# Setting the sign of the converted float64 weights in ScalarE's scaled copy instead of in a third VectorE operation

## The chip, the cores and the metric

The kernel runs on one core of one Trainium2 chip. The metric is the device time of one execution in microseconds. Engines are called by the profile's names: PE (matrix multiplies), DVE (vector), ACT (scalar, activations), POOL (GpSimd) and SP (here only a queue that issues transfers).

## The reference

The inputs `q`, `k`, `v`, `p` are float32, all weights are float64. What is computed, cut to its core:

```python
p_packed = sm_attn(p, k, v)                    # 8 x 8 heads, 32 packed rows, 576 keys, head size 64
x = sm_attn(q, p_packed, p_packed)             # then 4608 tokens x 512
g = x @ w_gate                                 # 512 -> 1536
x = (g * (1 / (1 + exp(-g))) * (x @ w_val)) @ w_out      # 1536 -> 512
return (((x @ w1) * (x @ w2)) @ w3) @ w_out2   # 512 -> 1024 -> 1024 -> 512
```

`sm_attn` scales by 1/8, subtracts the row's maximum, takes the exponential and divides by the row's sum plus 1e-9.

## The kernel before, in words

The program has four stages. **Front** (to about 111 us): sixteen units, one for each batch and half of the heads, load `k` and `v`, transpose on PE, and make the packed rows; its order is written out by hand as tasks at fractions of a unit (`task`, `run`), and each engine runs its part in that order. **P = 0** (to about 250 us): the first of four batch pairs; twelve steps `f`, each with the gate and value products of 128 columns (`stage1`, lines 440 to 473), a combination of weights with packed rows (`c_mm`, tile `pc`, then `ch` and `cl`), and after each third step the output product (`stage3`, tiles `px` and `acc`). **P = 1 to 3** (to about 840 us): the same steps with weights that were stored to DRAM; in P = 3 the products `w3 @ w_out2` (`w3_T`, `w3_mm`) are put between. **Tail**: the second MLP. From the front's end on, a scheduler sets each engine's order by its own estimate of when work is ready, so an instruction can move when another is shortened or goes away.

[...] `conv` (line 334) turns each tile of 128 x 512 numbers into float32 from its two 32-bit words, `high` and `low`. ACT multiplies `high`, taken as a float32, by 2^-112 (L347), into the target tile `t`; DVE shifts `low` right by 29 into `x` (`vx`, L350); DVE shifts `t` left by 3 and joins `x` (L357). The shift throws the sign away. It is put back in one of two ways: behind the front by DVE with the top bit of `high` (L360), and in the front by an ACT `Sign` (L354) and a POOL multiplication (L363), spread over two later times of the hand-written order (`CVD`).

There are 76 such tiles: `w` (gate and value, 24, target `wf`), `wo` (12, target `wof`), `w12` (16), `wo2` (8) and `w3` (16, targets `vt`). Six of them, `wf` 0 to 2, are converted in the front, 24 + 12 - 6 = 30 in P = 0 or just ahead of it, the rest later. In P = 0, `c_mm` of step `f` needs `wf` of step `f`, which is converted two steps ahead. The raw tiles have five buffers; a load on the SP queue waits until a buffer's last reader is done.

Of the kernel before, what the change touches and what calls it, by code (L numbers as in the profile page):

```python
# [8 lines left out]
F32 = mybir.dt.float32  # L9
F32R = mybir.dt.float32r  # L10
I32 = mybir.dt.int32
I64 = mybir.dt.int64
AF = mybir.ActivationFunctionType
ALU = mybir.AluOpType
# [5 lines left out]
VD = 0  # L20
RAW0 = (7, 8, 10, 11, 12, 13, 15, 15, 15, 16.75)
WS = {10.0: (0, 0), 11.0: (0, 1), 13.25: (1, 0), 14.25: (1, 1), 15.25: (2, 0), 16.25: (2, 1)}
CVD = (0.25, 1.25)
SPD = 2.25
CS = (13, 16)
CO = (14.0, 17.0)
# [4 lines left out]
QD = ((0, 'load'), (4.0, 'T'), (5.25, 'mm'), (6.0, 'max'), (6.0, 'sub', 'pool'), (6.75, 'exp'), (7.25, 'sum'), (7.75, 'div', 'pool'), (8.75, 'aT', 'later'), (9.5, 'split'))  # L31
STD = 4.75
W3B = 5
DSIGN = ('w',)
SIGN = -(1 << 31)
W3S = ((0, 1, 2, 3), (1, 3), (1, 3))
NPS = 0

# [2 lines left out]
def packed_attention_moe_kernel(  # L41
# [24 lines left out]
    nc = tc.nc  # L66
# [16 lines left out]
    scale = 1.0 / float(D) ** 0.5  # L83

    def pool(name, side, bufs=1, **kw):
        return tc.alloc_tile_pool(name=name, bufs=bufs, side=side, reuse_waits="tile", **kw)
# [30 lines left out]
    vc = pool("vc", "left", bufs=2)  # L117
# [18 lines left out]
    in_front, conv_rest, pin, pin_at = [True], [], {}, {}  # L136
    NO_SYNC = mybir.DependencyInfo(mybir.DependencyClass.NoSync, mybir.DependencyReason.DATA)

    def behind(x, what):
        if what in pin:  # L140
            tc.add_manual_dep(x.ins, pin[what].ins.name, NO_SYNC, reason="behind the last unit")
# [176 lines left out]
    def raw_load():  # L318
        if raw_at[0] < len(raw_q):
            key = raw_q[raw_at[0]]  # L320
            src = raw_src(key)
            raw_at[0] += 1
            blocks = src.shape[0] == 4
            t = vc.tile([128, 512] if blocks else [128] + list(src.shape[1:]), I64, tag="raw",
                        name=f"raw_{key}", bufs=5)
            if blocks:
                for i in range(4):
                    to = t[32 * i:32 * i + 32]
                    nc.sync.dma_start(to if len(src.shape) == 3 else to.rearrange("p (r n) -> p r n", r=4), src[i])
            else:  # L330
                nc.sync.dma_start(t, src)
            raw_t.append((key, t))

    def conv(key, t):


        name, raw = raw_t.pop(0)
        assert name == key, (name, key)
        x = vc.tile(list(t.shape), I32, tag="vx", name=f"vx_{key}")
        w = raw.bitcast(I32)  # L340
        if len(t.shape) == 3:
            w = w.rearrange("p a (n e) -> p a n e", e=2)
            low, high = w[:, :, :, 0], w[:, :, :, 1]
        else:
            w = w.rearrange("p (n e) -> p n e", e=2)
            low, high = w[:, :, 0], w[:, :, 1]
        behind(nc.scalar.activation(t, high.bitcast(F32), AF.Copy, scale=2.0 ** -112), "act")  # L347
        dve = not in_front[0] and key.startswith(DSIGN)
        sg = None if dve else vc.tile(list(t.shape), F32, tag="sg", name=f"sg_{key}")
        behind(nc.vector.tensor_scalar(x, low, 29, None, op0=ALU.logical_shift_right), "dve")  # L350

        def sign():
            if not dve:
                nc.scalar.activation(sg, high.bitcast(F32), AF.Sign)  # L354

        def rest():
            nc.vector.scalar_tensor_tensor(  # L357
                x, t.bitcast(I32), 3, x, op0=ALU.logical_shift_left, op1=ALU.bitwise_or)
            if dve:
                nc.vector.scalar_tensor_tensor(  # L360
                    t.bitcast(I32), high, SIGN, x, op0=ALU.bitwise_and, op1=ALU.bitwise_or)
            else:
                nc.gpsimd.tensor_tensor(out=t, in0=x.bitcast(F32), in1=sg, op=ALU.mult)  # L363

        if in_front[0]:
            conv_rest.extend((sign, rest))
        else:
            sign()
            rest()
        if not in_front[0]:  # L370
            raw_load()
# [4 lines left out]
    def w_conv(f, gv):  # L376
        if gv == 0:
            wf_t[0, f] = wst_t[f] = wgv.tile([128, 4, 2, 128], F32, tag=("wh", "wl")[f % 2], name=f"wf0_{f}")
        t = wf_t[0, f]
        conv(f"w_{f}_{gv}", t[:, :, gv, :])  # L380
# [11 lines left out]
    def wo_conv(f):  # L392
        t = vl.tile([128, DM], F32, tag="vt", name=f"wof0_{f}")
        conv(f"wo_{f}", t)
        wof_t[0, f] = t
# [123 lines left out]
    def pa_s(u):  # L519


        kT = kT_t.pop(u)
        t = psum(f"psp{u}")
        for hq in range(4):
            for e in range(2):
                es = slice(64 * e, 64 * e + 64)
                nc.tensor.matmul(
                    t[hs[hq], e, 0:HS].rearrange("j (m p g) -> j g m p", m=3, g=3), lhsT=kT[es, 9, hs[hq]],
                    rhs=kT[es, 0:9, hs[hq]].rearrange("d (g m) p -> d g m p", g=3), start=True, stop=True, tile_position=(64 * e, 32 * hq))
        mx = pa.tile([128, 1], F32, tag="mx", name=f"mx{u}")  # L530
        nc.vector.reduce_max(mx, t[:, :, 0:HS], axis=AX.XY)
        nc.vector.tensor_scalar_mul(mx, mx, -scale)
        return t, mx
# [57 lines left out]
    def task(s, fn, *args):  # L591
        extra.setdefault(s, []).append((fn, args))
# [7 lines left out]
        task(s, raw_load)  # L600
    for s, (f, gv) in WS.items():
        task(s, w_conv, f, gv)
        for d in CVD:
            task(s + d, lambda: conv_rest.pop(0)())
    C_t["later"] = [None]
    for f in range(2):
        task(CS[f] + 0.5, c_mm, 0, f)
# [10 lines left out]
    with tc.manual_schedule(engines=M0):  # L618
        for s in range(last + 1):
# [6 lines left out]
            if 0 <= s - 1 < U:  # L626
                x = pa_s(s - 1)
# [61 lines left out]
    def w12_conv(i):  # L689
        x, c, h = w12_list[i]  # L690
        t = vl.tile([128, 512], F32, tag="vu", name=f"w12t{i}")
        conv(f"w12_{i}", t)
        nc.sync.dma_start(
            w12d[4 * h:4 * h + 4, :, x, c, :].rearrange("f p n -> p f n"),
            t.rearrange("p (f n) -> p f n", n=128))
# [408 lines left out]
```

## Time and profile before

| | us |
|---|---|
| median of 3 runs | 1408.45 (1404.53 to 1416.2) |
| the profiled execution, its own time | 1409.99 |
| its span, first to last instruction | 1408.2 |
| PE busy | 1356.6 (96%) |
| DVE busy | 715.9 (51%) |
| ACT busy | 577.0 (41%) |
| POOL busy | 400.6 (28%) |

Busy times are sums over the whole span, and the stages have different limits; the granted clock of PE was 0.99 of full speed in the mean. A matmul row's length depends on that clock, so a stretch of half clock shows as longer rows, not as idle time.

### The profile page before, as it was taken

How to read it: one execution, taken by the hardware profiler on the slowest of the kernel's cores; microseconds unless marked ns; L12 is line 12 of the kernel's file. 1: busy time of each engine (PE TensorE's matmuls, PEld its weight loads, DVE VectorE, ACT ScalarE, POOL GpSimd, SP SyncE). 2: the span in 40 equal slices, each digit the busy share in tenths (PEclk: the TensorE clock that was granted, in tenths of full speed). 3: DMA queues.
4: the chain of work that ended last, by engine and by line, in shares of the span. 5: the costliest groups of instructions: out<-in, count | busy, mean ns of one | idle time of the engine just before them, and what ended most of it. 6: DMA issues, size and time to landing. Idle time of an engine off the chain costs nothing.

```text
span 1408.2 us, 25693 instructions
## 1 busy us (share of the span) xinstructions
PE 1356.6 (96%) x10228; PEld 1243.6 (88%) x10228; DVE 715.9 (51%) x1016; ACT 577.0 (41%) x946; POOL 400.6 (28%) x315
## 2 busy tenths in 40 slices
PE   7779989999999999999999989999999999999998
PEld 5557988999999999998988889989999899898997
DVE  3557769536584566664265467933323323334130
ACT  5585525435243353354453234623323323233231
POOL 0244223332223323254243334602212022021120
PEclk9999999999999999999999999999999999999999
DMA  9997567543446534235442137946728458185451
GB/s 255 252 253 195 196 177 238 137 154 85 137 107 179 174 101 135 59 118 153 133 145 88 61 109 254 337 167 195 224 85 254 148 162 253 59 252 174 133 158 45
DMA packets 188871, 230.28 MB, mean 164 GB/s; under 512 B 70736, under 2 KB 119888, under 8 KB 188752
## 3 DMA queue, kind: packets, MB, share of 16 engines
q1 hardware_dynamic: 188752, 228.64, 54.6%
q8 instruction: 81, 1.33, 0.4%
q14 instruction: 38, 0.31, 0.1%
HBM read 179.04 MB, written 49.55 MB: 162 GB/s over the span
## 4 chain that ended last, share of the span: by engine, by line
PE 77%; DVE 8%; DMA 6%; issue 4%; ACT 3%; POOL 1%; SPq 0%; DVEq 0%; ACTq 0%; POOLq 0%
PE px L668 19%; PE po L1041 14%; PE pA L977 12%; PE pg L454 8%; PE pv L454 8%; PE pB L977 6%; PE pC L977 3%; PE pc L422 3%; DMA km<-in_k_dram 2%; PE pw L732 1%; DMA raw_w<-in_moe_w_val_dram 1%; PE pk L512 1%; DVE vx_w L357 1%; DVE ws L90 1%; PE psq L207 1%
## 5 line engine op out<-in xcount | busy, mean ns | idle before, releaser
L90 POOL TENSOR_TENSOR ul<-u,uh 128x576 fp32r<-128x576 f32 x96 | 153.7, 1601 | 344.5 <-ACT uh L94 333.0
L997 POOL TENSOR_TENSOR c<-s,s 128x384 f32<-128x384 f32 x48 | 49.2, 1025 | 375.9 <-ACT s L992 375.7
L668 PE MATMUL px<-uh,woh 128*128 128x384 f32 x576 | 147.6, 336 | 3.2 <-DVE acc L678 2.2
L668 PE MATMUL px<-ul,woh 128*128 128x384 f32 x576 | 147.3, 336 | 2.6 <-POOL ul L90 2.6
L668 PE MATMUL px<-uh,wol 128*128 128x384 f32 x576 | 146.9, 336 | 0.0
L992 ACT COPY s<-pA 128x384 f32<-128x384 f32 x144 | 69.2, 481 | 181.7 <-PE pA L977 179.2
L463 DVE TENSOR_TENSOR u<-u,pv 128x576 f32<-128x576 f32 x96 | 71.8, 748 | 97.7 <-PE pv L454 83.2
L94 ACT CAST uh<-u 128x576 fp32r<-128x576 f32 x96 | 64.7, 674 | 134.7 <-DVE u L463 134.7
L1041 PE MATMUL po<-wo_hi,abl 128*128 128x512 f32 x288 | 112.3, 390 | 0.2 <-DVE abl L90 0.2
L1041 PE MATMUL po<-wo_lo,abh 128*128 128x512 f32 x288 | 112.2, 389 | 0.0
L1041 PE MATMUL po<-wo_hi,abh 128*128 128x512 f32 x288 | 112.0, 389 | 0.0
L668 PEld LDWEIGHTS px<-uh,woh 128*128 128x128 f32 x576 | 103.2, 188 | 5.9 <-DVE acc L678 2.8
L678 DVE TENSOR_TENSOR acc<-acc,px 128x768 f32<-128x768 f32 x72 | 68.1, 948 | 77.4 <-PE px L668 77.2
L668 PEld LDWEIGHTS px<-ul,woh 128*128 128x128 f32 x576 | 104.5, 188 | 3.1 <-POOL ul L90 3.1
L668 PEld LDWEIGHTS px<-uh,wol 128*128 128x128 f32 x576 | 104.6, 189 | 0.0
L90 DVE TENSOR_TENSOR abl<-ab,abh 128x768 fp32r<-128x768 f32 x48 | 48.1, 1003 | 105.1 <-ACT abh L94 105.1
L90 POOL TENSOR_TENSOR wol<-wof,woh 128x512 fp32r<-128x512 f32 x48 | 63.7, 1340 | 99.6 <-ACT woh L94 86.2
L454 PE MATMUL pg<-aTh,ch 128*128 128x288 f32 x384 | 87.9, 310 | 2.2 <-ACT u L459 2.2
L454 PE MATMUL pv<-aTh,ch 128*128 128x288 f32 x384 | 83.3, 299 | 2.9 <-ACT u L459 2.6
L459 ACT ACTIVATE u<-pg 128x576 f32<-128x576 f32 x96 | 62.3, 649 | 54.1 <-PE pg L454 53.2
L454 PE MATMUL pv<-aTl,ch 128*128 128x288 f32 x384 | 82.8, 298 | 0.0
L454 PE MATMUL pg<-aTh,cl 128*128 128x288 f32 x384 | 82.8, 297 | 0.0
(312 smaller groups left out, 3190.4 us busy)
## 6 DMA issues: line engine op xcount, KB each, us to landing
ws<-wsd SPq DMA_DIRECT2D x245, 256.0 KB, 3.0
wf<-Wd SPq DMA_DIRECT2D x36, 512.0 KB, 4.5
wsd<-ws SPq DMA_DIRECT2D x49, 256.0 KB, 3.5
km<-in_k_dram SPq DMA_DIRECT2D x16, 576.0 KB, 12.7
wof<-wod SPq DMA_DIRECT2D x36, 256.0 KB, 3.2
x2r<-X2d SPq DMA_DIRECT2D x24, 384.0 KB, 5.2
out_dram<-o SPq DMA_DIRECT2D x36, 256.0 KB, 2.0
raw_w<-in_moe_w_dram SPq DMA_DIRECT2D x16, 512.0 KB, 4.9
```

The lines of the kernel that those rows point to most:

```text
L90: return eng.tensor_tensor(out=out, in0=src, in1=hi.bitcast(F32), op=ALU.subtract)
L94: nc.scalar.copy(hi, src)
L422: nc.tensor.matmul(t[hs[at], b, Q], lhsT=PTd[es, 2 * (2 * P + b) + Q, hs[hq]], rhs=w[es, 2 * Q + hq // 2].rearrange("p g n -> p (g n)"), s ...
L454: nc.tensor.matmul(t[:, hf, 0:HS], lhsT=w[:, b % 2, Q, cols], rhs=x[:, Q, hf, :], start=first, stop=last,)
L459: x = nc.scalar.activation(u, t[:, :, 0:HS], AF.Silu)
L463: x = nc.vector.tensor_tensor(out=u, in0=u, in1=t[:, :, 0:HS], op=ALU.mult)
L668: nc.tensor.matmul(t[:, h, 0:CW], lhsT=w[:, 128 * d:128 * d + 128], rhs=x[:, CW * c:CW * c + CW], start=first, stop=last,)
L678: nc.vector.tensor_tensor(out=o, in0=o, in1=t[:, :, 0:CW], op=ALU.add)
L977: nc.tensor.matmul(bk[n], lhsT=w[:, hl, 128 * d:128 * d + 128], rhs=r[:, d], start=(first and d == 0 and i == 0), stop=(d == 1 and i == 2) ...
L992: nc.scalar.copy(o, t)
L997: on.tensor_tensor(out=r, in0=o, in1=t, op=op)
L1041: nc.tensor.matmul(t, lhsT=a[:, j, cols], rhs=w[:, f], start=first, stop=last)
```

## The change

ACT's scaled copy becomes a `Prelu` with slope -2^32. A positive high word gives the same as before. A negative one gives its magnitude, 32 binades up: bit 28 of the word is then set, and the shift left by 3 moves it to the sign's place. The third DVE operation, the `Sign` and the POOL multiplication are gone, as are the tiles `sg`; the joining operation now writes `t` in place. In the front it stands a quarter of a unit behind its load's task, where before it stood one and a quarter behind.

```diff
-CVD = (0.25, 1.25)
+CVD = 0.25
...
-        behind(nc.scalar.activation(t, high.bitcast(F32), AF.Copy, scale=2.0 ** -112), "act")
-        dve = not in_front[0] and key.startswith(DSIGN)
-        sg = None if dve else vc.tile(list(t.shape), F32, tag="sg", name=f"sg_{key}")
+        behind(nc.scalar.activation(t, high.bitcast(F32), AF.Prelu, scale=2.0 ** -112, alpha=-2.0 ** 32), "act")
         behind(nc.vector.tensor_scalar(x, low, 29, None, op0=ALU.logical_shift_right), "dve")
-
-        def sign():
-            if not dve:
-                nc.scalar.activation(sg, high.bitcast(F32), AF.Sign)
 
         def rest():
             nc.vector.scalar_tensor_tensor(
-                x, t.bitcast(I32), 3, x, op0=ALU.logical_shift_left, op1=ALU.bitwise_or)
-            if dve:
-                nc.vector.scalar_tensor_tensor(
-                    t.bitcast(I32), high, SIGN, x, op0=ALU.bitwise_and, op1=ALU.bitwise_or)
-            else:
-                nc.gpsimd.tensor_tensor(out=t, in0=x.bitcast(F32), in1=sg, op=ALU.mult)
+                t.bitcast(I32), t.bitcast(I32), 3, x, op0=ALU.logical_shift_left, op1=ALU.bitwise_or)
 
         if in_front[0]:
-            conv_rest.extend((sign, rest))
+            conv_rest.append(rest)
         else:
-            sign()
             rest()
...
-        for d in CVD:
-            task(s + d, lambda: conv_rest.pop(0)())
+        task(s + CVD, lambda: conv_rest.pop(0)())
```

In all, the DVE has 70 instructions fewer, ACT six and POOL six; the number of activation table loads in the program is 16 before and after. PE's order is the same. Two places of the order matter below. First DVE in P = 0, between `wf` of step 6 and `wf` of step 7 (`cl` is the remainder of `pc`, `aT` and `aTl` belong to the attention of the next batch). Before:

```order
L360 SCALAR_TENSOR_TENSOR wf_6_2272<-raw_w_1_2023,vx_w_1_2280 128x4x128
L350 TENSOR_SCALAR vx_wo_2320<-raw_wo_2030 128x512
L463 TENSOR_TENSOR u_4_2288<-u_4_2288,pv_4_2303 128x576
L357 SCALAR_TENSOR_TENSOR vx_wo_2320<-wof_4_2319,vx_wo_2320 128x512
L261 STREAM_TRANSPOSE aT_0_2636<-sT_1947 128x576
L360 SCALAR_TENSOR_TENSOR wof_4_2319<-raw_wo_2030,vx_wo_2320 128x512
L90 TENSOR_TENSOR cl_6_2351<-pc_6_2333,ch_6_2350 128x1024
```

And in the changed kernel, the same stretch:

```order
L349 SCALAR_TENSOR_TENSOR wf_6_2244<-wf_6_2244,vx_w_1_2251 128x4x128
L449 TENSOR_TENSOR u_4_2211<-u_4_2211,pv_4_2226 128x576
L346 TENSOR_SCALAR vx_wo_2290<-raw_wo_2003 128x512
L88 TENSOR_TENSOR aTl_2598<-aT_0_2599,aTh_2597 128x576
L349 SCALAR_TENSOR_TENSOR wof_4_2289<-wof_4_2289,vx_wo_2290 128x512
L449 TENSOR_TENSOR u_4_2258<-u_4_2258,pv_4_2273 128x576
L259 STREAM_TRANSPOSE aT_1_2603<-sT_1922 128x576
L88 TENSOR_TENSOR aTl_2598<-aT_1_2603,aTh_2597 128x576
L88 TENSOR_TENSOR cl_6_2320<-pc_6_2302,ch_6_2319 128x1024
```

The two L360 are gone. Both `aTl` and the second `aT`, which stood behind `wf` of step 7, now stand ahead of it; the first `aT` moved further up, ahead of `cl` of step 5.

Second, ACT somewhat earlier in P = 0, at the exponential of the next batch's attention (`sT`), among the output copies `acc` of the first `stage3`. Before:

```order
L674 COPY acc_3_2174<-px_0_3_2155 128x768
L94 CAST woh_3_2136<-wof_3_2127 128x512
L674 COPY acc_4_2195<-px_0_4_2176 128x768
L239 ACT_TABLE_LOAD
L239 ACTIVATE sT_1947<-sT_1947 128x1152
```

In the changed kernel:

```order
L659 COPY acc_3_2146<-px_0_3_2127 128x768
L92 CAST woh_3_2108<-wof_3_2100 128x512
L237 ACT_TABLE_LOAD
L237 ACTIVATE sT_1922<-sT_1922 128x1152
L659 COPY acc_4_2167<-px_0_4_2148 128x768
```

The table load and the exponential moved ahead of one `acc` copy.

## Rows read from the trace of the kernel before

**Rows 1.** Stretches: us, each engine's busy time (instructions), PE clock, DMA share, GB/s

```profile
250.00:574.00 324.00, 324.00 (x2811) 302.57 (x2810) 194.73 (x230) 132.53 (x190) 102.40 (x71) 1.00 0.48 135
...
180.00:185.00 5.00, 4.46 (x43) 3.34 (x44) 4.85 (x8) 2.73 (x4) 2.56 (x2) 0.50 0.87 278
```

**Rows 2.** Timeline of PE: start, length, instruction, [idle before it, and what ended that]

```profile
130.06 1.16 PE L207 MATMUL psq<-qT,PTd 64*32 64x288 f32 x12 [0.41 <-DVE qT L158]
132.86 1.10 PE L422 MATMUL pc<-wf,PTd 64*32 64x256 f32 x32 [1.64 <-DVE wf L360]
...
169.26 1.10 PE L422 MATMUL pc<-wf,PTd 64*32 64x256 f32 x32 [1.01 <-DVE wf L360]
...
180.53 1.96 PE L422 MATMUL pc<-wf,PTd 64*32 64x256 f32 x32 [3.58 <-DVE wf L360]
...
228.95 1.10 PE L422 MATMUL pc<-wf,PTd 64*32 64x256 f32 x32 [1.54 <-DVE wf L360]
...
647.07 0.53 PE L454 MATMUL pv<-aTh,ch 128*128 128x288 f32 x2 [2.58 <-ACT u L459]
...
716.19 0.53 PE L454 MATMUL pg<-aTh,ch 128*128 128x288 f32 x2 [2.23 <-ACT u L459]
...
744.04 0.62 PE L668 MATMUL px<-uh,woh 128*128 128x384 f32 x2 [1.94 <-DVE acc L678]
```

**Rows 3.** The chain that ended last, PE's pieces: start, length, what

```profile
182.50 3.18 PE pg L454 x12
185.68 2.10 PE pv L454 x12
...
197.16 1.60 PE pg L454 x12
...
647.07 2.93 PE pv L454 x12
```

**Rows 4.** Groups by line and shape: count | busy us, mean ns | idle before

```profile
L360 DVE SCALAR_TENSOR_TENSOR wf<-raw_w,vx_w 128x512 int32<-128x512 int32 x18 | 13.2, 751 | 0.0
L357 DVE SCALAR_TENSOR_TENSOR vx_w<-wf,vx_w 128x512 int32<-128x512 int32 x24 | 17.7, 753 | 0.1
L347 ACT ACTIVATE wf<-raw_w 128x512 f32<-128x512 f32 x24 | 15.6, 673 | 6.1 <-DMA raw_w<-in_moe_w_gate_dram 5.0 <-DMA raw_w<-in_moe_w_val_dram 1.1
L354 ACT ACTIVATE sg_w<-raw_w 128x512 f32<-128x512 f32 x6 | 4.0, 675 | 0.0
L459 ACT ACT_TABLE_LOAD x8 | 10.3, 1283 | 2.7 <-PE pg L454 2.6
```

**Rows 5.** Stretches, line L360 alone: us, DVE busy (instructions), PE clock, DMA

```profile
111.30:132.90 21.60, 3.93 (x6) 1.00 0.56 154
160.80:180.50 19.70, 3.88 (x5) 0.98 0.53 158
215.80:229.00 13.20, 2.72 (x4) 1.00 0.71 220
634.00:647.00 13.00, 2.16 (x2) 1.00 0.56 178
```

**Rows 6.** Timeline of DVE and ACT in P = 0

```profile
157.21 1.94 DVE L234 TENSOR_TENSOR sT<-sT,qmx 128x1152 f32<-128x1152 f32 x1
...
159.66 1.17 ACT L239 ACTIVATE sT<-sT 128x1152 f32<-128x1152 f32 x1
...
182.18 0.74 DVE L90 TENSOR_TENSOR aTl<-aT,aTh 128x576 fp32r<-128x576 f32 x1
```

**Rows 7.** Timeline of DVE and ACT late in the front

```profile
94.04 0.68 DVE L357 SCALAR_TENSOR_TENSOR vx_w<-wf,vx_w 128x512 int32<-128x512 int32 x1
...
94.62 0.69 ACT L347 ACTIVATE wf<-raw_w 128x512 f32<-128x512 f32 x1
```

**Rows 8.** The chain that ended last, in P = 3

```profile
733.30 1.96 DVE vt_w L360
...
737.12 3.59 DMA raw_w<-in_moe_w_dram
```

More of the change, by code (lines that the diff above doesn't have):

```diff
@@ L33 @@
 W3B = 5
-DSIGN = ('w',)
-SIGN = -(1 << 31)
 W3S = ((0, 1, 2, 3), (1, 3), (1, 3))
```

## The prediction, as it was put on record

> **What bounds the kernel now.** I read the stretches first, to see where PE is ever idle; then PE's timeline for each gap and what ended it; then the chain of waits backwards from each gap, to see whether a removed operation is on it. PE bounds the program: from 250 to 574 us it is busy 324.00 of 324.00 us [rows 1]. Nothing that is taken from DVE there can show in the time. What a change of DVE can win is PE's gaps, and there are few. Eight of them matter [rows 2]. Four are ended by L360 itself, the operation that goes: 1.64, 1.01, 3.58 and 1.54 us, each the matmul `pc` that waits for `wf`, all in P = 0. One of 0.41 us stands just before the first, behind a DVE transpose in the same rush. Three are in P = 3: 2.58 us and 2.23 us ended by ACT's `u`, 1.94 us ended by DVE's `acc`. In P = 0 DVE is the late engine, while elsewhere it has room.
>
> A gap costs more than its length when the clock drops behind it. Behind the 3.58 us gap the stretch 180 to 185 was granted 0.50 of full speed [rows 1], the lower of the two levels: `pc` took 1.96 us where others take 1.10 [rows 2], and the twelve matmuls of `pg` and `pv`, 1.60 us at full speed, took 3.18 and 2.10 us [rows 3]. That is 0.86 + 1.58 + 0.50 = 2.94 us on top. Behind the 2.58 us gap `pv` took 2.93 us, 1.33 more than 1.60 [rows 3]. Behind the 1.54 us gap `pc` took the usual 1.10 us [rows 2].
>
> **The change part by part.** *The third DVE operation goes.* 70 of them, 0.751 us each in the form of `wf` [rows 4], some 52 us of DVE time; only what lies on the way to one of the gaps counts.
>
> (a) 130 to 133 us, idle 0.41 + 1.64 = 2.05 us. Between the front's end and this gap DVE runs six L360, 3.93 us [rows 5]. Part of that is hidden where DVE waits for ACT, but the two of them for `wf` of step 4 lie behind those waits and the `wof` pair is what ACT itself waits for. I take the gap as closed: 2.05 us.
>
> (b) 169 and 180.5 us, idle 1.01 + 3.58 = 4.59 us. The stretch begins with the end of the exponential (159.66 + 1.17 us [rows 6]), and from there DVE has no pause until the second gap ends. Five L360 go, 3.88 us [rows 5]. The exponential itself comes earlier: DVE's subtraction ahead of it ends at 157.21 + 1.94 = 159.15 us [rows 6] and has two L360 ahead of it (2 x 0.68, taken with the shortest price, 0.68 us, as L357 had at 94.04 us [rows 7]: 1.36), and ACT no longer does one `acc` and the table load between. So it starts near 157.8, not 159.66: 1.8 us. Against that, the order puts two `aTl` and one `aT` ahead of `wf` of step 7: three operations near 0.74 us [rows 6], 2.2 us. Net 3.88 + 1.8 - 2.2 = 3.4 us of the 4.59; some 1.2 us of idle time stays. As a gap of 1.54 us kept the full clock, I take the 2.94 us of slow clock as gone. Together 6.3 us.
>
> (c) 229 us, idle 1.54 us. Four L360, 2.72 us, between 215.8 and 229 us [rows 5]; the first stands behind a load's landing and the others behind each other. Closed: 1.54 us.
>
> (d) 647 us, idle 2.58 us and 1.33 us of clock, 3.91 us. Two L360 with 2.16 us lie between 634 and 647 us [rows 5]; through `acc` and its store they hold the SP queue, on which the load of `wof` stands, which ACT's cast and then `u` wait for. The scheduler has moved casts and loads here too, so I take half: 2.0 us.
>
> (e) 744 us, idle 1.94 us. A raw load landed here after 3.59 us [rows 8]; its buffer came free when L360 at 733.30, 1.96 us long, had read `high` [rows 8]. Now the last readers are the Prelu and the shift, which stand earlier than L360, so the load starts at least that much sooner. Closed: 1.94 us.
>
> (f) 716 us, idle 2.23 us: the way there goes over POOL's `w3l` and the one buffer of `w3T`, not over L360. Nothing.
>
> *Prelu for Copy.* The trace of before has no Prelu. Nearest are the same shape as scaled copy, 0.673 us, and as `Sign`, 0.675 us [rows 4], the latter a function that also treats the two signs apart. I take 0.675; 76 x 0.002 us is nothing. *The joining operation in place.* It reads what L357 reads and writes where L360 wrote: 0.753 and 0.751 us [rows 4], no difference. *Front.* Six `Sign` (4.0 us on ACT [rows 4]) and six POOL products go; the joining operation stands a unit earlier. The front hangs on its loads and ACT, so I take nothing for it either way.
>
> Sum: 2.05 + 6.3 + 1.54 + 2.0 + 1.94 = 13.9 us. Against the profiled execution's 1410.0 that is **1396**; this execution stands 1.5 us above the median of the runs shown.
>
> **The rivals.** *Everything closes*: (b) and (d) in full, 2.05 + 4.59 + 2.94 + 1.54 + 3.91 + 1.94 = 17.0, and perhaps (f): 1391 to 1393. Chance 0.09.
>
> *New waits take the old ones' place*, chance 0.27. With DVE early, the next late ones are ACT's casts and `u` and the loads of raw tiles. For it: the long gaps (b) and (d) have several engines on their way, and the order moved there. Against it: ACT was busy 2.73 of 5 us in the worst stretch [rows 1]. Only (a), (c) and (e) are won: 1410 - 5.5 = 1404.5.
>
> *The change frees nothing*: the gaps stay in other names, 1410 within 2 us. Against it speaks that four gaps name L360 itself. Chance 0.06.
>
> *The front gets slower*, the other side. The joining operation now follows its Prelu within the unit. Where DVE comes to it before ACT has done the Prelu, DVE stands, and the maximum or the sum's reciprocal and `Pd` of the packed rows stand behind it, which PE waits for. In the trace DVE would be there at 94.04 us, the copy ended at 94.62 + 0.69 = 95.31 [rows 7]: 1.3 us. If all six tiles lost that on the path, 7.6 us; if also nothing were won later, 1418. It decides when ACT lags in most of the six, and by the rows it lags in that one. Chance 0.04. With the later gains it gives 1404.
>
> *Table loads*, also slower. If Prelu were not in the function table that is active, each one between exponentials or Silus would need a load and a load back, 1.283 us each [rows 4]: for the six of the front, where ACT is the tight engine, 6 x 2.57 = 15 us, 1425, and more in P = 0. It decides with the count of loads, and the program has 16 before and after. Chance 0.02. [...]
>
> *The change does not do what it says*: the removed operations are gone from the order, and what is left of this case lies within "frees nothing".
>
> **How the numbers follow.** The forecast, 1396, with its own range 1392 to 1400, has 0.52; everything closed 0.09, new waits 0.27, nothing 0.06, the slow ones 0.06. The 80% range reaches from 1389 (everything closed, and a run below the median like the 1404.5 of before) to 1409. A measurement of this kernel can tell about 1%, 14 us, from no change. The forecast sits on that bound: half of it, and all of "everything closes", count as faster by over 1%, 0.26 + 0.09 = 0.35, with 0.02 for a lucky front: 0.37. Slower by over 1% is 0.05, within 1% the rest, 0.58.
>
> **What would show it.** Right: the gaps before `pc` at the places of (a) to (c) are gone or under 1.5 us, no stretch of P = 0 is granted 0.5, and 250 to 574 is shifted but as long as before. Prelu rows at 0.67 to 0.68 us and 16 table loads. The raw load ahead of (e) issued before, not behind, the last DVE operation on its buffer's old tile. Wrong: PE's gaps of P = 0 as long as before with ACT or a load as what ended them; a front that ends later than 111 us; more than 16 table loads; or gaps in the stretch 250 to 574, which has none.

## The result, and the profile after

The changed kernel took 1391.08 us, median of 6 runs (1388.83 to 1397.78), beside 1409.62 (1404.53 to 1416.26) of the kernel before. The ratio is 0.987 (0.9833 to 0.9907). Its profiled execution took 1395.48 us with a span of 1393.5: 14.7 us shorter than the span of before, and 4.4 us above its own median. One execution of e3 (2202.28 us) and one of e7 (2694.21 us) below fell in a slow state; the ratios leave them out, the medians have them in.

PE still bounds the program, and DVE lost 59.9 us of busy time, from 715.9. First the page of the changed kernel, busy time of each engine:

```profile
PE 1351.7 (97%) x10228; PEld 1240.4 (89%) x10228; DVE 656.0 (47%) x946; ACT 574.4 (41%) x940; POOL 384.4 (28%) x309
```

Then its groups by line and shape, which answer to [rows 4]. L345 is the line of the copy, now the Prelu; L349 is the joining operation, now in place; L445 holds eight of the table loads:

```profile
L349 DVE SCALAR_TENSOR_TENSOR wf<-wf,vx_w 128x512 int32<-128x512 int32 x24 | 17.7, 747 | 2.1 <-ACT wf L345 2.0
L345 ACT ACTIVATE wf<-raw_w 128x512 f32<-128x512 f32 x24 | 15.5, 674 | 14.2 <-DMA raw_w<-in_moe_w_gate_dram 9.9 <-DMA raw_w<-in_moe_w_val_dram 4.4
L445 ACT ACT_TABLE_LOAD x8 | 10.3, 1283 | 1.4 <-PE pg L440 1.3
```

The Prelu takes 674 ns, where the copy took 673. The program has 16 table loads, as before, so the rival with table loads is out. No load was added where the Prelu stands between two exponentials (at 89.89 us, between those at 83.53 and 92.43) or two Silus (at 125.71 us, between those at 125.18 and 126.61).

PE's timeline of the changed kernel answers to [rows 2]: the three gaps that are left in P = 0, a new one of 1.40 us, and the one that is left at (f). In brackets is the idle time and what ended it:

```profile
129.34 0.45 PE L205 MATMUL psq<-qT,PTd 64*32 64x288 f32 x4 [0.63 <-DVE qT L156]
...
172.37 0.53 PE L440 MATMUL pv<-aTh,ch 128*128 128x288 f32 x2 [0.73 <-DVE cl L88]
...
175.00 1.10 PE L408 MATMUL pc<-wf,PTd 64*32 64x256 f32 x32 [0.77 <-ACT uh L92]
...
619.59 0.62 PE L653 MATMUL px<-uh,woh 128*128 128x384 f32 x2 [1.40 <-DVE acc L663]
...
701.24 0.52 PE L440 MATMUL pg<-aTh,ch 128*128 128x288 f32 x2 [1.21 <-ACT u L445]
```

No `pc` waits for `wf` any more. The gaps of 1.64, 1.01, 3.58 and 1.54 us in P = 0 are gone, and so are those of 2.58 us (647 us) and 1.94 us (744 us) in P = 3. What these rows show is shorter than any gap that the slow clock followed behind the front in either profile (3.58, 2.58 and 1.63 us before, 1.63 us after).

Two gaps do not fit the picture of gaps that close. The one of 1.40 us is new: no such gap stands ahead of this `px` in the kernel before, in e1 or in e5. And at the end of P = 3 gaps of 0.74, 0.22, 0.99 and 1.63 us stand in a row ahead of `px` pieces, in both kernels. Before:

```profile
839.09 0.69 PE L668 MATMUL px<-ul,woh 128*128 128x384 f32 x1 [1.63 <-POOL ul L90]
```

In the changed kernel it is 1.63 us at 821.89 us, ended by `ul` too, and the clock granted behind it was 0.51 of full speed from 822 to 825 us (before: 0.50 from 839 to 842).

PE runs the same instructions in the same order in both kernels and in every experiment below, so the program can be cut at the same matmuls: the first `pc` behind the front, the start of three later `px` pieces (in the kernel before 118.53, 233.44, 574.32 and 839.09 us), and the end. The stretch called P = 3 begins a little earlier, in the last part of P = 2. These are the stretches of the two kernels: start and end, length, then busy time of PE, PE's weight loads, DVE, ACT and POOL (instructions), PE's granted clock, DMA share, GB/s. Before:

```profile
0.00:118.53 118.53, 91.10 (x1544) 67.44 (x1545) 58.26 (x145) 74.21 (x132) 30.73 (x29) 0.94 1.03 248
118.53:233.44 114.91, 106.59 (x942) 96.19 (x942) 88.98 (x121) 55.72 (x84) 38.08 (x26) 0.97 0.64 187
...
574.32:839.09 264.77, 252.79 (x1860) 231.66 (x1859) 140.20 (x174) 112.18 (x158) 100.70 (x68) 0.99 0.34 104
```

After:

```profile
0.00:117.59 117.59, 89.91 (x1544) 67.19 (x1544) 56.85 (x140) 71.32 (x127) 23.23 (x25) 0.94 1.04 254
...
117.59:223.01 105.42, 103.30 (x942) 94.34 (x942) 74.97 (x101) 56.32 (x85) 33.58 (x24) 1.00 0.69 205
223.01:564.01 341.00, 341.00 (x2913) 319.50 (x2913) 183.24 (x229) 141.16 (x198) 106.87 (x73) 1.00 0.50 140
564.01:821.89 257.88, 251.27 (x1860) 230.54 (x1858) 123.33 (x152) 112.01 (x158) 98.92 (x68) 1.00 0.36 107
```

P = 0 lost 9.49 us: idle time fell from 8.32 to 2.12 us (length less PE's busy time), and PE's busy time fell by 3.29 us for the same 942 matmuls, which is the clock, from 0.97 to 1.00. The middle kept its length, 341 us, with some 28 us less of DVE in it: PE has no idle time there, so nothing could be won. P = 3 lost 6.89 us, 5.37 of idle time and 1.52 of PE's busy time, the new gap already taken off. The tail became 2.5 us longer, 571.6 for 569.1; below, it lies between 569 and 572 in every kernel.

### The profile page after: what moved, and what is told of

The parts are those of the page before. It is cut to its first block, busy times and chain, and to the rows that moved or that the text cites. A ratio compares the mean times of both kernels' runs of the same rounds, so it can differ in the third digit from the quotient of the medians.

```text
span 1393.5 us, 25570 instructions
## 1 busy us (share of the span) xinstructions
PE 1351.7 (97%) x10228; PEld 1240.4 (89%) x10228; DVE 656.0 (47%) x946; ACT 574.4 (41%) x940; POOL 384.4 (28%) x309
## 4 chain that ended last, share of the span: by engine, by line
PE 80%; DVE 2%; POOL 2%; DMA 1%; issue 1%; ACT 1%; SPq 0%; DVEq 0%; POOLq 0%; ACTq 0%
PE px L653 19%; PE pA L962 14%; PE po L1026 14%; PE pg L440 9%; PE pv L440 8%; PE pB L962 7%; PE pC L962 3%; PE pc L408 3%; PE pw L717 2%; PE psq L205 1%; POOL ul L88 0%; DMA wo3r<-wo3d 0%; POOL wo2l L88 0%; DMA x2r<-X2d 0%; DVE x2T L787 0%
## 5 line engine op out<-in xcount | busy, mean ns | idle before, releaser
L88 POOL TENSOR_TENSOR ul<-u,uh 128x576 fp32r<-128x576 f32 x96 | 146.0, 1521 | 333.2 <-ACT uh L92 328.2
L445 ACT ACTIVATE u<-pg 128x576 f32<-128x576 f32 x96 | 62.4, 651 | 59.8 <-PE pg L440 58.2
## 6 DMA issues: line engine op xcount, KB each, us to landing
ws<-wsd SPq DMA_DIRECT2D x245, 256.0 KB, 3.1
wsd<-ws SPq DMA_DIRECT2D x49, 256.0 KB, 3.0
wof<-wod SPq DMA_DIRECT2D x36, 256.0 KB, 3.0
out_dram<-o SPq DMA_DIRECT2D x36, 256.0 KB, 2.0
```

The lines of the kernel that those rows point to most:

```text
L88: return eng.tensor_tensor(out=out, in0=src, in1=hi.bitcast(F32), op=ALU.subtract)
L445: x = nc.scalar.activation(u, t[:, :, 0:HS], AF.Silu)
```

## The experiments

Theory A is that of the prediction for P = 0: DVE's own time, operation by operation, is on the way to PE's gaps. The rival for P = 3, step (e) of the prediction, is that raw tiles' buffers come free sooner, so that loads start sooner. All stretches, in us, each from one profiled execution; ratio and median from the timed runs:

| kernel | front | P = 0 | middle | P = 3 | ratio to before | median |
|---|---|---|---|---|---|---|
| before | 118.5 | 114.9 | 340.9 | 264.8 | | 1409.62 |
| changed | 117.6 | 105.4 | 341.0 | 257.9 | 0.987 (0.9833 to 0.9907) | 1391.08 |
| e1, third operation back | 115.9 | 113.6 | 340.9 | 265.2 | 0.9989 (0.9958 to 1.0019) | 1409.83 |
| e2, the same, reads the raw tile | 113.7 | 113.4 | 340.9 | 269.3 | 1.0021 (0.9995 to 1.0048) | 1414.86 |
| e3, changed in the front only | 126.3 | 115.9 | 340.9 | 266.2 | 1.0014 (0.9986 to 1.0043) | 1414.99 |
| e4, changed behind it only | 118.2 | 105.4 | 341.0 | 258.2 | 0.9896 (0.9857 to 0.9934) | 1397.46 |
| e5, changed in P = 0 only | 117.0 | 105.4 | 340.9 | 266.3 | 0.9924 (0.9896 to 0.9953) | 1401.75 |
| e6, changed in P = 1 to 3 only | 114.9 | 113.7 | 341.0 | 258.4 | 0.992 (0.9895 to 0.9944) | 1400.86 |
| e7, two operations back | 119.7 | 125.0 | 341.1 | 269.4 | 1.0118 (1.0089 to 1.0148) | 1428.77 |
| e8, changed, once more | 113.5 | 105.4 | 341.0 | 258.4 | 0.9888 (0.9854 to 0.9923) | 1396.33 |
| e9, one operation a tile | 114.2 | 102.7 | 341.4 | 256.0 | 0.9857 (0.9813 to 0.99) | 1388.18 |
| e10, raw tiles held | 111.9 | 107.6 | 341.5 | 258.9 | 0.9928 (0.9895 to 0.9961) | 1400.9 |

The kernel before, run beside them, had medians of 1412.67 (e1 to e4), 1412.65 (e5 to e8) and 1411.03 (e9, e10). The front is between 111.9 and 126.3 us long, and 117.6 and 113.5 in two executions of the same changed kernel, so nothing under some 5 us can be read from one profile's front. The times in the expectations count from a before of 1409.6 us; the before beside e1 to e8 stood 3 us higher, so the ratios are what is compared.

**e1, a third DVE operation put back, of the same shape, but reading `x` and not the raw tile.** It changes no value; the raw tile's buffer comes free as early as in the changed kernel.

```diff
             nc.vector.scalar_tensor_tensor(
                 t.bitcast(I32), t.bitcast(I32), 3, x, op0=ALU.logical_shift_left, op1=ALU.bitwise_or)
+            if not in_front[0]:
+                for _ in range(1):
+                    nc.vector.scalar_tensor_tensor(
+                        t.bitcast(I32), x, 0, t.bitcast(I32), op0=ALU.bitwise_and, op1=ALU.bitwise_or)
```

> Changed kernel with a third DVE operation put back behind the front, on 70 tiles: it joins the target with x and 0, so it changes nothing, is as long as L360 and, unlike it, does not read the raw tile. Theory A (the gain is DVE time on the way to PE's gaps): the gaps of P = 0 and P = 3 come back, the time is 1403 to 1409 (before 1409.6, changed 1391.1; some 2 us may stay from the front). Theory B (raw buffers come free earlier, loads start earlier): the time stays within 4 us of 1391. Theory C (the front's six Sign and POOL products): within 4 us of 1391 too, since the front is as changed. In A the gap ahead of pc near 175 us is over 2 us long, in B and C under 1.

The whole gain went. PE's gaps in P = 0 came back at the same matmuls and with the same lengths (1.64, 1.01, 3.58 us), now ended by L353, the operation put back; the fourth, 1.54 us, came back at 225.04 us. PE's timeline of e1:

```profile
130.24 1.10 PE L412 MATMUL pc<-wf,PTd 64*32 64x256 f32 x32 [1.64 <-DVE wf L353]
...
166.62 1.10 PE L412 MATMUL pc<-wf,PTd 64*32 64x256 f32 x32 [1.01 <-DVE wf L353]
...
177.89 1.10 PE L412 MATMUL pc<-wf,PTd 64*32 64x256 f32 x32 [3.58 <-DVE wf L353]
```

P = 0 and P = 3 of e1:

```profile
115.90:229.54 113.64, 105.31 (x942) 95.61 (x942) 88.96 (x121) 55.71 (x84) 38.12 (x26) 0.98 0.63 188
...
570.41:835.61 265.20, 252.86 (x1859) 231.85 (x1859) 141.20 (x174) 112.02 (x158) 100.15 (x68) 0.99 0.34 104
```

The gaps of P = 3 came back too, one of them that of step (e), 744 us in the kernel before. Waits of PE in P = 3 of e1: us in total, times, longest:

```profile
PE px L657 <- DVE acc L667: 2.4, 2, 2.1
PE pv L444 <- ACT u L449: 2.4, 1, 2.4
PE pg L444 <- ACT u L449: 2.2, 1, 2.2
```

The raw buffers of e1 were free early, and the gap ahead of `px` was there all the same. The rival is refuted for that gap. The chain of e1 that ends with it has no load between 724 us and the gap:

```profile
729.71 1.87 DVE vt_w L353
...
734.08 1.17 ACT w3h(1, 1)_8604 L92
...
735.31 1.57 POOL w3l(1, 1)_8605 L88
...
739.58 0.96 DVE acc L667
```

`acc` stands in DVE's queue behind the conversions and behind the transpose `w3T`, for which DVE waits 1.42 us until POOL's `w3l` is done. What makes `acc` late is DVE's queue, with its own operations and that wait in it.

**e2, the same with the raw tile as operand,** so that its buffer is held as in the kernel before.

```diff
-                        t.bitcast(I32), x, 0, t.bitcast(I32), op0=ALU.bitwise_and, op1=ALU.bitwise_or)
+                        t.bitcast(I32), high, 0, t.bitcast(I32), op0=ALU.bitwise_and, op1=ALU.bitwise_or)
```

> As the run before, but the third operation reads the raw tile's high word, so that it holds the buffer as L360 did. Theory A: within 2 us of the run before, since the loads were not what was late. Theory B: 1405 to 1410 here, while the run before is near 1391. A mixture gives the share: the step between these two runs is the price of the held buffers; I expect it in P = 3 alone (the gap before px near 744 us) and 1 to 2 us.

The medians are 5.0 us apart, where theory A allowed 2: a miss, though the intervals of the two ratios overlap. In the profile its P = 3 was 4.1 us longer than that of e1, and 3.4 of that are PE's busy time for the same matmuls (256.24 for 252.86 us), which is the clock (0.98 for 0.99): behind its gaps of 2.09 us (711 us) and 2.1 us (741 us) the twelve matmuls of `pg` took 3.25 us and the 54 of `px` 11.23, where e1, behind the same two gaps of 2.23 and 2.1 us, took 1.85 and 9.63. The gap of step (e), 2.1 us, was no longer than that of e1, so the step of 1 to 2 us that was expected there did not come. Whether held buffers cost anything is asked again by e10.

**e3, the change in the front alone, and e4, the change behind the front alone.** Both from the kernel before, with the two ways of conversion side by side (the operations behind the copy follow the way chosen):

```diff
+        pre = in_front[0]          # e3; e4: not in_front[0]
+        if pre:
+            behind(nc.scalar.activation(t, high.bitcast(F32), AF.Prelu, scale=2.0 ** -112, alpha=-2.0 ** 32), "act")
+        else:
             behind(nc.scalar.activation(t, high.bitcast(F32), AF.Copy, scale=2.0 ** -112), "act")
```

> Kernel before with Prelu for the six tiles of the front alone; behind the front everything as before. The changed profile reached the first pc behind the front 0.9 us earlier than the profile of before. Theory A: 1407.5 to 1409.5, a gain of 0 to 2 us. Theory C: over half of the gain, 1400 or less.

> Kernel before with Prelu for the 70 tiles behind the front alone; the front keeps Copy, Sign and the POOL product. Theory A: nearly the whole gain, 1390 to 1394. Theory C: under half of it, 1400 or more. If the parts add, this gain and the gain of the front alone sum to that of the change, 18.5 us in the medians.

The front's part is worth nothing that can be measured, though it takes six `Sign` and six POOL products away: 2 us were lost by the ratio, with an interval from 6 lost to 2 won. The part behind the front is the change. By the ratios the two add up to 12.7 us, for 18.3 of the change and 15.8 in e8; each has an interval of 4 to 5 us to either side, so the sum is no sharp test. The front's length varies with the rate of its transfers, as two profiles show, e3's and then that of e8, the changed kernel run once more: about the same bytes came at 234 and at 263 GB/s, with a DMA share of 1.00 and over in both. That the loads set the front's length is likely by these rows, and not shown by an experiment.

```profile
0.00:126.28 126.28, 91.72 (x1545) 69.26 (x1545) 59.63 (x145) 71.32 (x127) 21.54 (x24) 0.93 1.00 234
```

```profile
0.00:113.52 113.52, 88.27 (x1544) 65.34 (x1545) 56.84 (x140) 71.61 (x127) 23.27 (x25) 0.97 1.05 263
```

**e5, the change in P = 0 alone, and e6, in P = 1 to 3 alone.**

```diff
-        pre = not in_front[0]
+        pre = not in_front[0] and key.split("_")[0] in ("w", "wo")       # e5
+        pre = key.split("_")[0] in ("w12", "wo2", "w3")                  # e6
```

> Kernel before with Prelu for the tiles of w and wo behind the front (30 tiles, P = 0) alone. Between the first pc behind the front and the last px of P = 0 the changed profile won 9.5 us on that of before. Theory A, by place: this gain and no other, 8 to 10 us, ratio 0.993 to 0.994, with P = 3's gaps (2.6, 2.2, 1.9 us) as before. Rival D (the gaps are one debt: what P = 0 wins is lost again in P = 3, or the other way round): under 4 us or over 14.

> Kernel before with Prelu for w12, wo2 and w3 (40 tiles, P = 1 to 3) alone. In the changed profile the stretch from 574 us of before to the end of P = 3 was 6.9 us shorter, and the tail gave back 2.3. Theory A, by place: 4 to 7 us, ratio 0.995 to 0.997, with the four gaps before pc in P = 0 at 1.64, 1.01, 3.58 and 1.54 us as before. Rival D: under 2 us or over 10.

Each wins its own stretch, and that alone. P = 0 and P = 3 of e5:

```profile
117.00:222.41 105.41, 103.28 (x942) 94.35 (x942) 74.89 (x101) 56.28 (x85) 33.58 (x24) 1.00 0.70 205
...
563.31:829.65 266.34, 254.56 (x1859) 232.83 (x1858) 141.11 (x174) 112.19 (x158) 100.20 (x68) 0.99 0.34 103
```

The same of e6:

```profile
114.92:228.57 113.65, 105.33 (x942) 95.64 (x942) 88.96 (x121) 55.69 (x84) 38.08 (x26) 0.98 0.65 189
...
569.54:827.97 258.43, 251.28 (x1860) 230.63 (x1859) 123.50 (x152) 112.21 (x158) 98.98 (x68) 1.00 0.35 107
```

By the stretches the two gains are in different places, and each is as large alone as together: 9.5 us of P = 0 and 6.3 of P = 3 (6.4 in e8, 6.9 in the first profile). The timed runs do not show that as well: 10.7 us for e5 and 11.3 for e6 by the ratios are 22.0 together, 6.2 more than the 15.8 of e8 beside them, where the expectation of e8 allowed 4. Each of the three has an interval of 3.5 to 5 us to either side. The ratio of e5, 0.9924, is just past the 0.993 to 0.994 that was expected. The time of e6 was a clear miss: 4 to 7 us less was expected, and 0.992 of the 1412.65 beside it is 11.3 us less (7.9 to 14.8 by the interval). Its P = 3 shrank by 6.3 us, as expected; the rest is within what front and tail vary by.

**e7, two DVE operations put back:** `range(2)` in the edit of e1, four operations a tile.

> Changed kernel with two DVE operations put back behind the front instead of one, so one more than before had. Theory A: DVE is the late engine in P = 0, so every operation more is paid in full there: the four gaps before pc grow by the further operation's 0.68 us times those on the way, together by 9 to 14 us; with P = 3 the time is 1420 to 1432, 10 to 20 us over before. Theory E (the schedule's order, not the engine's time, made before slow): within 5 us of before.

P = 0 of e7, and PE's waits in it:

```profile
119.74:244.76 125.02, 108.53 (x942) 97.29 (x942) 104.69 (x144) 57.13 (x84) 37.83 (x24) 0.96 0.60 183
```

```profile
PE pc L412 <- DVE wf L353: 16.4, 5, 5.2
```

PE is idle for 16.5 us there (length less busy time), and 16.4 of them are ended by DVE's last operation on `wf`. The 15.7 us of DVE time that a further operation adds to P = 0 of e1 (88.96 to 104.69) cost 11.4 us of time. The rival that the order of the schedule, and not DVE's time, made the kernel before slow had given a time within 5 us of before; e7 is 16 us over it.

**e8, the changed kernel once more,** beside e5 to e7.

> The changed kernel once more beside these. Theory A: ratio 0.985 to 0.990; the gains of the two partial kernels of this call sum to its gain, less what the front gives, within 4 us.

The stretches of P = 0, the middle and P = 3 repeat within 0.5 us (105.39, 341.00 and 258.35).

**e9, one DVE operation a tile behind the front.** The shift of the low word goes, and with it the low word's three bits are left out of the weights.

```diff
-        behind(nc.vector.tensor_scalar(x, low, 29, None, op0=ALU.logical_shift_right), "dve")
+        if in_front[0]:
+            nc.vector.tensor_scalar(x, low, 29, None, op0=ALU.logical_shift_right)
...
+            if not in_front[0]:
+                nc.vector.scalar_tensor_tensor(
+                    t.bitcast(I32), t.bitcast(I32), 3, t.bitcast(I32),
+                    op0=ALU.logical_shift_left, op1=ALU.bypass)
+                return
```

> Changed kernel without the shift of the low word behind the front: one DVE operation a tile is left there (the low word's three bits are left out of the weights). So far the stretch from the first pc behind the front to the fourth px of P = 0's second pair was 125.0, 114.9 or 113.6, and 105.4 us with four, three and two operations, some 10 us for each. Theory A (DVE's time counts only until PE's gaps are shut): 3.6 us of idle time are left in that stretch of the changed kernel, so it falls by no more than that, to 102 to 105 us, P = 3 by no more than 4 us, and the time stays within 8 us of the changed kernel. Rival G (DVE still bounds P = 0): it falls by 8 to 10 us again, to 96 or 97.

P = 0 and P = 3 of e9:

```profile
114.16:216.85 102.69, 102.69 (x942) 94.13 (x942) 60.53 (x79) 55.24 (x84) 32.48 (x23) 1.00 0.71 210
558.27:814.22 255.95, 250.80 (x1859) 230.64 (x1858) 112.15 (x132) 112.08 (x158) 98.45 (x68) 1.00 0.36 108
```

PE is busy for the whole of P = 0: there is nothing more to win there. With one, two, three and four operations a tile P = 0 took 102.7, 105.4, 113.4 to 115.9 and 125.0 us. The third operation cost 8.0 to 10.5 us, the second 2.7: the gain of taking one away shrinks as the gaps run out, and the time of e9 is that of the changed kernel within the intervals.

**e10, the raw tiles held in the changed kernel** by a last reader of one column behind the joining operation:

```diff
+            if not in_front[0]:
+                t1, h1 = (t[:, 0, 0:1], high[:, 0, 0:1]) if len(t.shape) == 3 else (t[:, 0:1], high[:, 0:1])
+                nc.vector.scalar_tensor_tensor(
+                    t1.bitcast(I32), h1, 0, t1.bitcast(I32), op0=ALU.bitwise_and, op1=ALU.bitwise_or)
```

> Changed kernel with one more DVE operation of a single column a tile behind the front, which reads the raw tile's high word: the raw buffer is held as before, at hardly any DVE time (an operation of one column took 0.14 to 0.15 us in the trace of before). Step (e) of the prediction (the buffer that comes free earlier lets the raw load start earlier): the gap ahead of px near the end of P = 3's first half, 1.94 us before and gone in the changed profile, is back with 1 to 2 us, and the stretch of P = 3 is 259 to 262 us instead of 258. Theory A (DVE's time alone): no gap there over 0.5 us, P = 3 within 1 us of 258, P = 0 within 2 us of 105.4.

P = 0 and P = 3 of e10:

```profile
111.91:219.46 107.55, 104.57 (x942) 94.99 (x942) 76.70 (x121) 55.88 (x85) 34.51 (x25) 0.98 0.67 197
561.00:819.85 258.85, 251.31 (x1860) 230.56 (x1859) 127.44 (x174) 111.67 (x158) 99.00 (x68) 1.00 0.35 106
```

P = 3 stayed nearly as short as in the changed kernel (258.85 for 257.9 to 258.4), with the raw buffers held, and the `px` of step (e) did not wait: the longest wait for `acc` in P = 3 was 0.9 us, at another place (619.57 us).

```profile
PE px L657 <- DVE acc L667: 0.9, 1, 0.9
```

With e1 that settles step (e) from both sides. P = 0 has as many DVE instructions as before (121) and keeps most of the gain: what counts there is DVE's time, not the number of its operations. P = 0 was 2.1 us longer, just past the 2 us that theory A allowed, with one gap of 2.2 us ahead of `pc`. The added operation was not as small as meant, as two of its groups by shape show:

```profile
L353 DVE SCALAR_TENSOR_TENSOR w12t<-raw_w,w12t 128x1 int32<-128x1 int32 x16 | 16.7, 1042 | 0.3
L353 DVE SCALAR_TENSOR_TENSOR wf<-raw_w,wf 128x1 int32<-128x1 int32 x18 | 9.4, 533 | 0.0
```

DVE was busy 1.73 us longer in P = 0. The gap of 2.2 us is ended by a long one of them, on DVE's timeline and then in the chain:

```profile
168.58 1.35 DVE L353 SCALAR_TENSOR_TENSOR wf<-raw_w,wf 128x1 int32<-128x1 int32 x1
```

```profile
168.58 1.36 DVE wf L353
...
170.08 1.96 PE pc L412 x32
```

At the usual 0.15 us it would have ended 1.2 us earlier and left a gap near 1.0 us, by this estimate, where the changed kernel has 0.77. So the operation's own length explains most of the gap; a part of the held buffers in it is not shown. The 0.9928 is slower than the changed kernel's ratio in its middle, while the intervals overlap; its profile was the shortest of its seven executions (spans of 1391.6 to 1405.8), so the rows above do not show what the longer ones lost.

## Why the prediction was right, step by step

The steps, each as the shift of PE's work from one place to the next between the two profiled executions:

| step | predicted, us | measured, us |
|---|---|---|
| front | 0 | 0.9 |
| (a) 130 to 133 | 2.05 | 1.7 |
| (b) 169 and 180.5, with the clock | 6.3 | 5.6 |
| (c) 229 | 1.54 | 2.2 |
| middle | 0 | -0.1 |
| (d) 647 | 2.0 | 3.3 |
| (e) 744 and (f) 716 | 1.94 + 0 | 3.0 |
| from there to 839 | 0 | 0.6 |
| tail | 0 | -2.5 |
| sum | 13.9 | 14.7 |

**The sum came out, in part by luck.** 13.9 us were forecast and the two profiled executions differ by 14.7. Between the first `pc` behind the front and 839 us, where the steps lie, 16.3 us were won; the 0.9 of the front and the -2.5 of the tail, which lie within the scatter of both, bring that back to near the forecast. The median, 1391.08, lies below the forecast's own range of 1392 to 1400, and inside the wider one.

**The mechanism was right in P = 0.** The four gaps that named L360 were DVE's, and they closed. For (b) a residue of 1.2 us was left standing; the trace has 0.73 us, ended by DVE's `cl`, and 0.77, ended by ACT's `uh`. The clock term came as predicted: 3.29 us of PE's busy time in P = 0, where 2.94 were put down, and the mean granted clock of P = 0 is 1.00. The middle is shifted and has no gap. The price put on the removed operation was low, which the sum does not use: 70 at 0.751 us were to be some 52 us, the 70 L360 took some 68, and DVE lost 59.9.

**(d) was undersized.** Half of its 3.91 us was taken, since the scheduler had moved casts and loads there. The gap of 2.58 us went and with it its clock: from 630 us of before to 660 the shift grew by 4.9 us. Ahead of that, 1.6 us were lost to the new gap of 1.40 us: in DVE's new order `acc` stands there behind the transpose `w3T`, for which DVE waited 2.28 us until POOL's `w3l` was done. The 3.3 us of the table are what is left of the two. e1 and e5, with three operations a tile there, do not have the new gap; e4, e6 and e8 do.

**(e) had the right size and the wrong cause.** The prediction had the raw load start earlier as the buffer came free. e1 frees the buffers early and has the gap; e10 holds them and has not. `acc` is a DVE operation, and what stood in DVE's queue ahead of it made it late: the conversions, as in P = 0, and the transpose that waits for POOL's `w3l`. The row of the gap had named DVE as what ended it.

**(f) was put at nothing, and about 1 us was won:** the gap fell from 2.23 to 1.21. With the third operation back (e1) it is 2.2 again, with one operation a tile (e9) 1.0. The path was as predicted: in the kernel before, e1 and e10 DVE waits 4.1 to 4.6 us for POOL's `w3l` before it makes the `w3T` ahead of that gap. What was left out is that the order ahead of `w3l` moves when operations go. In the five profiles with the change in P = 3 (changed, e4, e6, e8, e9) POOL makes `wo2l` ahead of `ul` there, and the gap is 1.05 to 1.23 us; in the seven others, e10 among them with 2.11, `ul` comes first, and it is 2.09 to 2.50. The one-column operations of e10 took 0.15 to 0.16 us around that gap, so DVE's time is not what counts there. That the order is the cause is read off these twelve profiles; no run changed it alone.

**The rivals.** New waits took an old one's place once, 1.6 us ahead of (d); in P = 0 ACT's `uh` ends one gap of 0.77 us, and no load ends any there. That the front got slower is not seen: e3, with the front's part alone, stands at 1.0014 (0.9986 to 1.0043), and the front took 116.6 us in the mean of the eight profiles that have the changed front, 117.2 in the four that do not.

**The chances** gave "within 1%" the most, since 13.9 us lay on that bound; the median fell by 18.5 us, and by 16.3 in the other comparison (e8). The steps up to 839 us add up to 17.2; the 2.5 us that the tail gave back in the profiled execution lie within its scatter from kernel to kernel.

## What to carry to other kernels

A gap's row names the engine that ended it: where the operation to be removed runs on that engine, within the same rush, believe the row, and count every such gap. Where the scheduler sets the order anew, look for a new wait as well: here one of 1.6 us came. An operation taken from an engine that is not the bound pays by the gaps that it feeds (here 16 to 18 us of 60 us of DVE time), nothing where the bound engine has no idle time (here the middle, 341 us with 28 us less of DVE in it), and less with each further one, as the gaps run out (here 11.4, 8.0 to 10.5 and 2.7 us in P = 0). Putting the removed time back with an operation of the same shape that changes no value is the cheapest test of the cause, and two separate halves show by their stretches whether they are independent, even where the timed runs scatter too much to add up.

## What the runs showed of the hardware

**The clock's price behind an equal gap varied.** The gap of 3.58 us ahead of the same `pc` stands in the kernel before, e1, e3 and e6 (3.57 in e2). From the start of that `pc` to the next `px` it took 7.08, 5.85, 6.70, 5.86 and 5.67 us, where the changed kernel, at full clock, took 4.34: the price was 1.3 to 2.7 us. Whether there was one varied too: behind the gap of (f), the twelve matmuls of `pg` took 3.25 us in e2 (a gap of 2.09 us) and 1.85 in e1 (2.23), and the kernel before (2.23) was granted 1.00 from 716 to 720 us. Two stretches of e1 show the granted clock behind the gap of 3.58 us, back at full speed some 5 us behind it, while the kernel before still had 0.50 in 180 to 185 us [rows 1]:

```profile
179.00:182.00 3.00, 3.00 (x14) 3.00 (x15) 2.85 (x5) 2.81 (x5) 2.20 (x2) 0.56 0.75 238
182.00:185.00 3.00, 3.00 (x20) 3.00 (x19) 2.42 (x5) 2.45 (x5) 0.81 (x1) 0.87 0.84 133
```

Behind the new gap of 1.40 us and the 1.21 of (f) the changed kernel kept 1.00; behind the 1.63 us at the end of P = 3, the last of four gaps in a row, it was granted 0.51.

**Some DVE operations lasted until a POOL operation that was under way had ended.** The 70 one-column operations of e10 fall into two groups: 42 took 0.14 to 0.16 us, and 28 took 0.92 to 1.52, more than the 0.68 of a whole tile's operation. Each of the 28 started while a POOL operation was running and ended within 0.02 us of that one's end; of the 42, one started beside a POOL operation, 0.06 us before its end. In the kernel before, 20 of the 70 L360 took 1.23 to 1.99 us, and each of them ended 0.55 or 0.56 us behind the end of such a POOL operation; the other 50 took 0.64 to 0.69. Four of these started beside POOL too, at operations whose own rows are unusually long (2.66 and 4.79 us, where `ul` takes 1.60 in the mean). The L360 of 1.96 us at 733.30 us [rows 8] is one of the 20. Not every operation did so: in the kernel before, the additions `u` that started beside POOL took 0.74 to 0.76 us, like the rest (0.72 to 0.76). This is read off the times of the rows; no run changed POOL's work alone.

**The front's rate of transfers differed between executions,** 234 to 264 GB/s where 29.4 to 30.0 MB are moved (rate by length), and its length with it, 126.3 to 111.9 us.
